# A 64-byte row instead of an 8-byte row in the first mixture's token table

## The chip, the cores and the metric

The kernel runs on one core of a Trainium2 chip. The metric is device time in microseconds (us) from launch to end. A core has five engines that run their own instruction queues and wait for each other by semaphores: PE (matmul and transposes), DVE (vector), ACT (activations, copies out of PSUM), POOL (GpSimd: element work, and the indirect DMAs, which gather or scatter rows by a list of indices), and SP, which here only starts plain DMAs. All DMAs of a core, whoever starts them, are carried by the same 16 DMA engines. On-chip memory has 128 partitions (SBUF for tiles, PSUM for matmul results); DRAM holds inputs, outputs and the two tables that this document is about.

## What is computed

Attention inside chunks of 64 positions, then two mixtures of 8 experts on the 4608 rows that it leaves. Cut to what matters:

```
x = attention(q, k, v)                        # 8 x 8 heads x 576 x 64, softmax in chunks of 64
x = x.transpose(0, 2, 1, 3).reshape(4608, 512)

# first mixture: every token goes to one expert
logits = x @ w_gate + modality_bias[modality_id]        # 4608 x 8
e_idx = argmax(logits); gate_w = softmax(logits)[e_idx]
out[e_idx == e] = gate_w * (relu(x[e_idx == e] @ w1[e]) @ w2[e])

# second mixture: only tokens with x @ w_skip > 0, the others are passed on
```

w1 is 8 x 512 x 1024 and w2 is 8 x 1024 x 512, both in float32.

## The kernel before

The program has three stages on one time line. **Attention** takes tiles of 128 tokens, 36 of them, t = 0 to 35, some 5.5 us each. `load_qk` brings q and k for 256 tokens in a DMA each (or two, at the edge of a batch), up to four pairs of tiles ahead, into two buffers; `load_v` brings v for a batch of 576 tokens (4.5 tiles), one DMA for each head, into one of two buffers (`g.v0` and `vt1`), two heads in each tile. All of these are started by SP, in the order of the program, so a load whose buffer isn't free yet holds those behind it. POOL reorders q and k (`reorder`, L445), PE transposes them (L453), forms scores (L482), transposes the exponentials (L508) and multiplies by v (`emit_av`, L517), after which DVE divides (`emit_norm`, L527 to L533). Every four tiles the finished rows are stored to DRAM by SP (L648, 1 MB).

Beside the tiles, and dripped in between their instructions, `route` sends each group of four tiles (512 tokens, groups gi = 0 to 8) through the first mixture's gate. Its product is a table in DRAM, `g.tab[0]`. It has a slot for each place in each expert's list: `g.NR` = 8 x 4608 + 256 = 37120 rows of two 32-bit numbers, the token's index and its gate as float bits. A token's slot is the expert's base (e x 4608) plus its rank among the tokens of that expert so far, so tokens of one expert fill slots that follow each other. `tables` (L157) first fills both tables with the index 65536, which later gathers skip; this is put on SP's queue in one of the first tiles. Then `route` writes index and gate of 4 x 128 tokens into a tile `row` (128 partitions x 4 x 2) and scatters them by four indirect DMAs of 128 rows each, started by POOL (L588), 36 in all. A `row` tile comes from a pool with two buffers.

**The first mixture's steps** read the table: `load_ids_at` (L323) fetches 256 consecutive slots, row by row, into an `ids` tile, POOL gathers the 256 rows of x that they name (L334), PE runs the two products (L364, L1095) and the results are scattered back (L1002). The first expert's w1 is loaded and split already during attention (L615 to L625), its w2 at the end of it (L1285, split on ACT and DVE in L980 and L982). While the first mixture runs, its outputs are routed for the second, with a table of the same shape, `g.tab[1]`, scattered at L268. **The second mixture's steps** read that one.

What sets the order around the change: SP's queue in program order for the two fills, the loads and the stores; POOL's queue in program order for the element work of `reorder` and the scatters. There is no planner.

Of the kernel before, what the change touches and what calls it, by code (L numbers as in the profile page):

```python
# [11 lines left out]
I32 = mybir.dt.int32  # L12
# [8 lines left out]
P = 128  # L21
E = 8
OOB = 65536.0
# [108 lines left out]
def setup_late(nc, g, tmp, modality_id, modality_bias, w_gate2, w_skip):  # L132

    NT, NTILE, DM = g.NT, g.NTILE, g.DM
    md = tmp.tile([NTILE, P, 2], I32, name="md")
    nc.gpsimd.dma_start(
        out=md, in_=modality_id.bitcast(I32).rearrange("(t p w) -> t p w", p=P, w=2)
    )
    b01 = tmp.tile([P, 2, E], F32, name="b01")
    nc.gpsimd.dma_start(  # L140
        out=b01.rearrange("p m e -> p (m e)"),
        in_=modality_bias.rearrange("m e -> (m e)").unsqueeze(0).to_broadcast([P, 2 * E]),
    )
    wsm = tmp.tile([P, 4, E + 1], F32, name="wsm")
    nc.gpsimd.dma_start(out=wsm[:, :, 0:E], in_=w_gate2.rearrange("(a p) e -> p a e", p=P))
    nc.gpsimd.dma_start(
        out=wsm[:, :, E:E + 1], in_=w_skip.rearrange("(a p o) -> p a o", p=P, o=1)
    )


    blank = tmp.tile([P, g.NR // P, 2], I32, name="blank")
    nc.gpsimd.memset(blank[:, :, 0], int(OOB))
    nc.gpsimd.memset(blank[:, :, 1], 0)

    def tables():
        for t in g.tab:
            nc.sync.dma_start(out=t.rearrange("(p n) c -> p n c", p=P), in_=blank)  # L157

    nop = lambda: None

    mf = tmp.tile([NTILE, P], F32, name="mf")

    def bias():
        pm = g.ps_l.tile([P, P], F32, tag="l", name="pm")
        nc.tensor.transpose(pm[:, 0:NTILE], mf, g.ident[0:NTILE, 0:NTILE])
        m = tmp.tile([P, NTILE, 2], F32, name="m")
        nc.vector.tensor_copy(m[:, :, 1], pm[:, 0:NTILE])
        nc.vector.tensor_scalar(
            out=m[:, :, 0], in0=m[:, :, 1], scalar1=-1.0, scalar2=1.0, op0=ALU.mult, op1=ALU.add
        )  # L170
        t0 = tmp.tile([P, NTILE, E], F32, name="t0")
        sh = [P, NTILE, E]
        for i, dst in ((0, t0), (1, g.bias)):
            nc.vector.tensor_tensor(
                out=dst,
                in0=m[:, :, i:i + 1].to_broadcast(sh),
                in1=b01[:, i:i + 1, :].to_broadcast(sh),
                op=ALU.mult,
            )
        nc.vector.tensor_tensor(out=g.bias, in0=g.bias, in1=t0, op=ALU.add)  # L180

    def rows():

        pr = g.ps_l.tile([P, DM], F32, tag="l", name="pr")
        for a in range(4):
            nc.tensor.transpose(pr[0:E + 1, a * P:(a + 1) * P], wsm[:, a, :], g.ident)
        rw = tmp.tile([E + 1, DM], F32, name="rw")
        nc.scalar.copy(rw, pr[0:E + 1, :])
        nc.scalar.dma_start(out=g.rows, in_=rw)

    g.late = [lambda: nc.vector.tensor_copy(mf, md[:, :, 0])] + g.late + [tables, nop, bias, nop, nop, nop, rows]


# [127 lines left out]

def load_ids_at(nc, g, which, dst, r):
    return nc.sync.dma_start(  # L323
        out=dst, in_=g.tab[which][bass.ds(r, 256), :].rearrange("(h p) c -> p h c", p=P)
    )


# [45 lines left out]
def attention(ctx, tc, g, q, k, v, w_gate, w1, out, small):  # L373
# [3 lines left out]
    nc = tc.nc  # L377
# [21 lines left out]
    ps_t, ps_l, rt_p = g.ps_t, g.ps_l, g.rt  # L399
# [154 lines left out]
    def route(gi, wait=3, wait2=1):  # L554
        for _ in range(wait):
            yield
        ps = ps_l.tile([P, 4, NA, 32], F32, tag="l", name="ps_l2")
        for t in range(4):
            nc.tensor.transpose(ps[:, t].rearrange("p a e -> p (a e)"), g.lsb[:, t * P:(t + 1) * P], ident)
        yield  # L560
        lgt = rt_p.tile([P, 4, E], F32, tag="lgt", name="lgt")
        nc.vector.tensor_reduce(
            out=lgt, in_=ps[:, :, :, 0:E].rearrange("p t a e -> p t e a"), axis=AX.X, op=ALU.add,
        )
        yield
        nc.vector.tensor_tensor(out=lgt, in0=lgt, in1=g.bias[:, 4 * gi:4 * gi + 4, :], op=ALU.add)
        row = rt_p.tile([P, 4, 2], I32, tag="row", name="row")
        nc.gpsimd.tensor_copy(row[:, :, 0], g.tokid[:, 4 * gi:4 * gi + 4])
        yield
        hot = yield from gate_argmax(nc, g, rt_p, lgt, 4, row[:, :, 1:2].bitcast(F32))  # L570
        for _ in range(wait2):
            yield
        ps = ps_l.tile([P, 5, E], F32, tag="l", name="ps_r")
        ranks_mm(nc, g, ps, hot, 4)
        yield
        pos = rt_p.tile([P, 4], F32, tag="pos", name="pos")
        yield from ranks(nc, g, rt_p, ps, hot, 4, g.carry[0], pos)
        posi = rt_p.tile([P, 4], I32, tag="posi", name="posi")
        nc.vector.tensor_copy(posi, pos)
        yield  # L580
        if gi == GP:
            yield from pick(nc, g, 0)
            jobs.extend(first_jobs())
        if gi == NG - 2:
            yield from snap(nc, g, 0)
        sc = []
        for i in range(4):
            b = nc.gpsimd.indirect_dma_start(  # L588
                out=g.tab[0], out_offset=IOff(ap=posi[:, i:i + 1], axis=0),
                in_=row[:, i, :], in_offset=None, bounds_check=g.NR - 1, oob_is_err=False,  # L590
            )
            sc.append(apart(tc, b, sc + (g.eids if gi > GP else [])))
            if gi < NG - 1:
                yield
                yield
        if gi == NG - 1:
            yield from g.control(0)
        if gi > GP:
            g.scat += sc
        if gi == NG - 2:  # L600
            early_ids(nc, g, 0, g.idsE[1], 256)
# [110 lines left out]
    for t in range(NTILE):  # L712
# [19 lines left out]
        if t == NTILE - 3:  # L732
            nc.sync.dma_start(
                out=g.v0[:, 0:(E + 1) * DM],
                in_=g.rows.rearrange("e d -> (e d)").unsqueeze(0).to_broadcast([P, (E + 1) * DM]),
# [197 lines left out]
def experts(ctx, tc, g, w, out, tail):  # L933
# [37 lines left out]
    def load_ids(which, j):  # L971
        load_ids_at(nc, g, which, g.ids[j % g.NID], reg(g.ints[which], j, 1, g.NR - 256))
# [378 lines left out]
@with_exitstack  # L1351
def kernel(
    ctx, tc, q, k, v, modality_id, w_gate, modality_bias, w1, w2,
    w_skip2, w_gate2, w12, w22, out, dbg=None,
):
    nc = tc.nc
    g = K()
    g.NT, g.DM = out.shape
    g.NTILE = g.NT // P
    g.NS = (g.NT + E * 255) // 256  # L1360
    g.VIRT = g.NS + 1
    g.NID = 5
    g.NR = E * g.NT + 256
    g.ints, g.ctl = {}, {}
    KD, KF = g.DM // P, w1.shape[2] // P
    dram = ctx.enter_context(tc.tile_pool(name="dram", bufs=1, space=DRAM))
    g.rows = dram.tile([E + 1, g.DM], F32, name="rows")
    g.tab = [dram.tile([g.NR, 2], I32, name=f"tab{i}") for i in range(2)]
    g.const = ctx.enter_context(tc.tile_pool(name="const", bufs=1))
    g.rt = ctx.enter_context(tc.tile_pool(name="rt", bufs=2))  # L1370
    keep = ctx.enter_context(tc.tile_pool(name="keep", bufs=1))
    g.ps_t = ctx.enter_context(tc.tile_pool(name="ps_t", bufs=3, space=PSUM))
    g.ps_l = ctx.enter_context(tc.tile_pool(name="ps_l", bufs=1, space=PSUM))
    g.w1s = keep.tile([P, 2, KD, KF * P], F32R, name="w1s")
    g.x4 = [keep.tile([P, 4, g.DM], F32, name=f"x4{i}") for i in range(3)]
    g.xe = keep.tile([P, 2, g.DM], F32, name="xe")
    g.xTb0 = keep.tile([P, 2, KD, 256], F32R, name="xTb0")
    g.xT4 = keep.tile([P, 4, 4 * P], F32, name="xT4")
    g.lsb = keep.tile([P, 4 * P], F32, name="lsb")

    g.v0 = keep.tile([P, q.shape[2] // 64 * q.shape[1] * (q.shape[3] + 1)], F32, name="v0")
    g.w2g = g.v0[:, 0:(E + 1) * g.DM].rearrange("p (e d) -> p e d", e=E + 1)
    g.lg = keep.tile([P, 2, E + 1], F32, name="lg")
    g.idsP = keep.tile([P, 2, 2], I32, name="idsP")
    g.row = keep.tile([P, 2, 2], I32, name="rowP")
    g.ids = [keep.tile([P, 2, 2], I32, name=f"ids{i}") for i in range(g.NID)]
    g.idsE = [keep.tile([P, 2, 2], I32, name=f"idsE{i}") for i in range(3)]
    with tc.manual_schedule():
        setup(tc, g)
        with ExitStack() as st:  # L1390
            tail = attention(
                st, tc, g, q, k, v, w_gate, w1, out, (modality_id, modality_bias, w_gate2, w_skip2)
            )
        experts(ctx, tc, g, ((w1, w2), (w12, w22)), out, tail)
# [31 lines left out]
```

## Time and profile before

| what | value |
|---|---|
| median of 3 runs | 992.92 us (992.51 to 997.83) |
| the profiled execution, as timed | 994.69 us |
| its span, first to last instruction | 993.0 us |
| busy: PE, DVE, ACT, POOL | 924.4, 646.2, 363.5, 309.2 us |
| mean granted TensorE clock | 0.974 of full |
| DMA | 119.38 MB in 121945 packets |

The profile cuts the span into 40 slices of 24.8 us; the attention stage is the first eight or nine. In a window's row stand, after the stretch and its length, the busy time of PE, of PE's weight loads (PEld), DVE, ACT and POOL, each with its number of instructions, and then the granted clock (1.00 is 2.4 GHz, 0.50 is 1.2 GHz), the mean busy share of the 16 DMA engines (over 1 where their packets overlap) and the GB/s that they moved. In a timeline's row stand the start, the length, the engine, the line, the operation, what it writes and reads, and in brackets how long the engine was idle before it and what ended that.

### The profile page before, as it was taken

To read this page: it belongs to the slowest core of one execution; us is meant where nothing else is said; L and a number is where in the kernel's file an instruction comes from. 1 tells how busy PE (TensorE), PEld (TensorE's weight loads), DVE (VectorE), ACT (ScalarE), POOL (GpSimd) and SP (SyncE) were. 2 spreads that over 40 slices of the span, in tenths; PEclk is the share of its full clock that TensorE was granted. 3 is DMA by queue.
4 is the path that set the end of the run, shared out by engine and by line. 5 is a ranking of instruction groups with operands and counts; after the bars stand their busy time and mean duration, and the time that the engine had idled before them with its cause. 6 is when DMAs were issued, how large, how long until landed. Compare 5 with 4: busy or idle time off the path is not lost. (4 is left out here: it accounts for less than half of the span.)

```text
span 993.0 us, 19577 instructions
## 1 busy us (share of the span) xinstructions
PE 924.4 (93%) x6757; PEld 816.3 (82%) x6757; DVE 646.2 (65%) x1837; ACT 363.5 (37%) x627; POOL 309.2 (31%) x284
## 2 busy tenths in 40 slices
PE   7887888889999999999889999988898999999996
PEld 6776767669999999888679999878797997897995
DVE  6576566558887777798687787788246365624361
ACT  6675667642212222341331121232126154514150
POOL 6464456424422222222232223220412211112210
PEclk9999898999999999999999999998999999999999
DMA  9999999584711111161101116000716546611500
GB/s 201 223 210 202 194 220 226 106 224 101 241 45 45 45 43 45 44 194 45 46 25 56 46 45 235 25 27 13 237 44 216 210 135 242 223 46 57 192 18 16
DMA packets 121945, 119.38 MB, mean 120 GB/s; under 512 B 56141, under 2 KB 93053, under 8 KB 121602
## 3 DMA queue, kind: packets, MB, share of 16 engines
q1 hardware_dynamic: 106192, 82.21, 33.2%
q0 software_dynamic: 14464, 34.17, 10.6%
q8 instruction: 85, 1.39, 0.7%
q14 instruction: 130, 1.06, 0.4%
q10 hardware_dynamic: 1074, 0.54, 0.2%
HBM read 96.37 MB, written 26.38 MB: 124 GB/s over the span
## 5 line engine op out<-in xcount | busy, mean ns | idle before, releaser
L1095 PE MATMUL p<-w2s,hT 128*128 128x512 f32 x1392 | 326.3, 391 | 0.0
L1095 PEld LDWEIGHTS p<-w2s,hT 128*128 128x128 f32 x1392 | 257.7, 188 | 51.9 <-DVEq L1203 0.2
L364 PE MATMUL p<-xTb,w1s 128*128 128x256 f32 x2064 | 263.2, 286 | 12.2 <-DVEq L1316 5.3
L364 PEld LDWEIGHTS p<-xTb,w1s 128*128 128x128 f32 x2064 | 254.7, 193 | 17.3 <-DVE w1s L982 6.2
L1012 DVE CUSTOM_DVE_ANT_0 x<-x,v 128x512 f32<-128x512 f32 x333 | 209.0, 686 | 47.7 <-ACT x L995 37.7
L1002 POOL DMA_INDIRECT out_dram<-x,ids x56 | 62.1, 1110 | 270.4 <-DVE x L998 205.7
L1061 ACT ACTIVATE hT<-p 128x512 fp32r<-128x512 f32 x86 | 51.4, 598 | 210.2 <-PE p L364 202.7
L268 POOL DMA_INDIRECT tab<-rowP,posi x38 | 40.6, 1069 | 222.8 <-DVE idsP L1111 175.6
L1062 DVE SCALAR_TENSOR_TENSOR hT<-p,hT 128x512 fp32r<-128x512 f32 x86 | 58.8, 686 | 65.6 <-ACT hT L1061 42.1
L334 POOL DMA_INDIRECT x<-out_dram,ids x68 | 76.7, 1128 | 56.5 <-issue 28.8
L364 PE MATMUL p1t<-xTb,w1s 128*128 128x256 f32 x696 | 88.1, 283 | 0.0
L364 PEld LDWEIGHTS p1t<-xTb,w1s 128*128 128x128 f32 x696 | 85.2, 191 | 1.7 <-issue 1.7
L995 ACT ACTIVATE x<-p,ids 128x512 f32<-128x512 f32 x33 | 22.7, 688 | 145.1 <-PE p L1095 141.7
L464 ACT COPY kb<-ps_t 64x512 f32<-64x512 f32 x70 | 44.0, 628 | 52.9 <-PE ps_t L453 52.5
L982 DVE TENSOR_TENSOR w2s<-r,w2s 128x512 fp32r<-128x512 f32 x88 | 56.8, 686 | 5.0 <-ACT w2s L980 5.0
L588 POOL DMA_INDIRECT tab<-row,posi x36 | 36.5, 1015 | 69.4 <-issue 28.3
L980 ACT CAST w2s<-r 128x512 fp32r<-128x512 f32 x88 | 51.0, 619 | 16.7 <-issue 6.4
L350 DVE TENSOR_TENSOR xTb<-px,xTb 128x512 fp32r<-128x512 f32 x70 | 44.9, 681 | 11.1 <-ACT xTb L349 10.3
L998 DVE SCALAR_TENSOR_TENSOR x<-p,ids,x 128x512 f32<-128x512 f32 x23 | 17.2, 747 | 53.4 <-PE p L1095 48.6
L527 DVE TENSOR_SCALAR rs<-o_ps 128x8 f32<-128x8 f32 x36 | 6.0, 166 | 67.3 <-PE o_ps L517 67.2
L982 DVE TENSOR_TENSOR w1s<-r,w1s 128x1024 fp32r<-128x1024 f32 x40 | 46.4, 1221 | 2.5 <-ACT w1s L980 2.2
L482 PE MATMUL sc<-kb,Tq 128*64 128x128 f32 x576 | 42.0, 287 | 5.9 <-DVE r_d L203 2.5
(217 smaller groups left out, 1110.4 us busy)
## 6 DMA issues: line engine op xcount, KB each, us to landing
r<-in_moe_w_dram SPq DMA_DIRECT2D x18, 2048.0 KB, 10.2
out_dram<-x SPq DMA_DIRECT2D x9, 1024.0 KB, 9.3
k<-in_k_dram SPq DMA_DIRECT2D x11, 512.0 KB, 6.8
q<-in_q_dram SPq DMA_DIRECT2D x11, 512.0 KB, 8.8
vt<-in_v_dram SPq DMA_DIRECT2D x32, 144.0 KB, 7.3
r<-in_moe_w_dram POOLq DMA_DIRECT2D x2, 2048.0 KB, 15.4
v<-in_v_dram SPq DMA_DIRECT2D x24, 144.0 KB, 7.3
v<-rows SPq DMA_DIRECT2D x1, 2304.0 KB
```

The costliest lines, as they stand in the source:

```text
L334: return [nc.gpsimd.indirect_dma_start(out=x[:, h, :], out_offset=None, in_=src, in_offset=IOff(ap=ids[:, h, 0:1], axis=0), bounds_check=s ...
L350: nc.vector.tensor_tensor(out=t[:, 1, :, h * P:(h + 1) * P], in0=ps, in1=o.bitcast(F32), op=ALU.subtract)
L364: nc.tensor.matmul(ps, w1s[:, b, kk, f * P:(f + 1) * P], xt[:, a, kk, :], start=(i == 0), stop=(i == 3 * KD - 1),)
L464: eng(kb[u % 2][64 * j:64 * j + 64, sl, j, :].rearrange("p a (c r) -> p a r c", r=2), ps[64 * j:64 * j + 64],)
L482: nc.tensor.matmul(out=ps[64 * c:64 * c + 64, a, :, :], lhsT=T_[u][:, a, cs], rhs=kb[u % 2][:, a, :, cs], start=True, stop=True,)
L980: hi(s[:, 0, kk, :], r[:, kk, :])
L982: eng.tensor_tensor(out=s[:, 1, kk, :], in0=r[:, kk, :], in1=s[:, 0, kk, :].bitcast(F32), op=ALU.subtract)
L1002: b = nc.gpsimd.indirect_dma_start(out=out, out_offset=IOff(ap=ids[:, h, 0:1], axis=0), in_=o[:, h, :], in_offset=None, bounds_check=NT - ...
L1012: nc.vector.tensor_tensor_reduce(out=junk[i % 2], in0=x2[:, h, :], in1=w2g[:, i, :], scale=1.0, scalar=0.0, op0=ALU.mult, op1=ALU.add, acc ...
L1061: nc.scalar.activation(out=o, in_=ps, func=AF.Relu)
L1062: nc.vector.scalar_tensor_tensor(out=l, in0=ps, scalar=0.0, in1=o.bitcast(F32), op0=ALU.max, op1=ALU.subtract)
L1095: nc.tensor.matmul(ps, hT[:, a, f, h * P:(h + 1) * P], w2s[:, b, f, :], start=(f == 0 and i == 0), stop=(f == KF - 1 and i == 2),)
```

## The change

The first table's rows get 16 numbers instead of 2, 64 bytes instead of 8. The second table stays as it is. Four things follow from that in the code.

- The fill of the first table writes 37120 x 64 bytes = 2.38 MB instead of 0.30 MB. Its source is a smaller tile, `blank0` (29 rows of 16 numbers in each partition), that the DMA reads ten times over.
- Four more memsets on POOL: two for `blank0`, one for each of two `row4` tiles.
- The scatters of `route` take whole rows of 64 bytes from `g.row4`, two fixed tiles used in turn; the numbers 2 to 15 of a row stay zero.
- `load_ids_at` fetches the first two numbers of each row.

```
+    n = g.NR // P
+    m = next(i for i in range(10, 0, -1) if n % i == 0)
+    blank0 = tmp.tile([P, n // m, 16], I32, name="blank0")
+    nc.gpsimd.memset(blank0, 0)
+    nc.gpsimd.memset(blank0[:, :, 0], int(OOB))
+    for t in g.row4:
+        nc.gpsimd.memset(t, 0)
+
     def tables():
-        for t in g.tab:
-            nc.sync.dma_start(out=t.rearrange("(p n) c -> p n c", p=P), in_=blank)
+        nc.sync.dma_start(
+            out=g.tab[0].rearrange("(p m n) c -> p m (n c)", p=P, m=m),
+            in_=blank0.rearrange("p n c -> p (n c)").unsqueeze(1).to_broadcast([P, m, n // m * 16]),
+        )
+        nc.sync.dma_start(out=g.tab[1].rearrange("(p n) c -> p n c", p=P), in_=blank)
...
-        out=dst, in_=g.tab[which][bass.ds(r, 256), :].rearrange("(h p) c -> p h c", p=P)
+        out=dst, in_=g.tab[which][bass.ds(r, 256), 0:2].rearrange("(h p) c -> p h c", p=P)
...
-        row = rt_p.tile([P, 4, 2], I32, tag="row", name="row")
+        row = g.row4[gi % 2]
...
-    g.tab = [dram.tile([g.NR, 2], I32, name=f"tab{i}") for i in range(2)]
+    g.tab = [dram.tile([g.NR, (16, 2)[i]], I32, name=f"tab{i}") for i in range(2)]
...
+    g.row4 = [keep.tile([P, 4, 16], I32, name=f"row4{i}") for i in range(2)]
```

No instruction of PE, DVE or ACT is added, removed or moved. On SP the two fills keep their place. This is SP's queue around them before, and then with the change (`blank` and `blank0` are the source tiles, `tab` the tables, `k`, `q`, `vt` the loads):

```order
L425 DMA k<-in_k_dram 128x8x128
L425 DMA q<-in_q_dram 128x8x128
L157 DMA tab_58<-blank 128x580
L157 DMA tab_59<-blank 128x580
L425 DMA k<-in_k_dram 96x8x128
```

```order
L437 DMA k<-in_k_dram 128x8x128
L437 DMA q<-in_q_dram 128x8x128
L165 DMA tab_58<-blank_357 1280x1x464
L169 DMA tab_59<-blank 128x580
L437 DMA k<-in_k_dram 96x8x128
```

The first fill is now 1280 runs of 464 numbers, ahead of the same loads. On POOL four memsets come between the constants and the first `reorder` (before, then with the change):

```order
L146 DMA wsm<-in_moe_w_skip_dram 128x4x1
L152 MEMSET blank 128x290
L153 MEMSET blank 128x290
L445 TENSOR_TENSOR rk<-k,zero 128x8x2x64
L445 TENSOR_TENSOR rq<-q,zero 128x8x2x64
```

```order
L146 DMA wsm<-in_moe_w_skip_dram 128x4x1
L152 MEMSET blank 128x290
L153 MEMSET blank 128x290
L159 MEMSET blank_357 128x464
L160 MEMSET blank_357 128x29
L162 MEMSET row_87 128x64
L162 MEMSET row_88 128x64
L457 TENSOR_TENSOR rk<-k,zero 128x8x2x64
```

Everything behind them on POOL stands in the order of before; a scatter's row there reads 37120x16 instead of 37120x2.

## Rows read from the trace of the kernel before

**Rows 1.** The page's 40 slices of 24.8 us: DMA share in tenths, GB/s.

```profile
DMA  9999999584711111161101116000716546611500
GB/s 201 223 210 202 194 220 226 106 224 101 241 45 45 45 43 45 44 194 45 46 25 56 46 45 235 25 27 13 237 44 216 210 135 242 223 46 57 192 18 16
```

**Rows 2.** DMA issues of the whole run: number, KB each, median us to landing.

```profile
tab<-blank SPq DMA_DIRECT2D x2, 290.0 KB, 5.8
tab<-row,posi POOLq DMA_INDIRECT x36, 6.6
```

**Rows 3.** Timeline of POOL: a reorder, and two of the 36 scatters.

```profile
51.31 1.89 POOL L445 TENSOR_TENSOR rq<-q,zero 128x1024 f32<-128x1024 f32 x1 [0.19 <-POOL rk L445]
...
58.73 1.08 POOL L588 DMA_INDIRECT tab<-row,posi  x1 [5.39 <-issue]
...
131.87 0.97 POOL L588 DMA_INDIRECT tab<-row,posi  x1 [0.30 <-issue]
```

**Rows 4.** Windows of the attention stage; the last three columns are PEclk, DMA share, GB/s.

```profile
64.00:66.00 2.00, 2.00 (x24) 1.48 (x20) 0.03 (x1) 1.98 (x5) 1.75 (x1) 1.00 1.06 79
66.00:69.00 3.00, 2.31 (x31) 1.58 (x28) 1.45 (x5) 0.97 (x2) 2.23 (x4) 1.00 1.10 306
72.00:76.00 4.00, 2.37 (x41) 2.22 (x38) 3.90 (x11) 1.82 (x5) 1.79 (x2) 1.00 1.20 136
94.00:100.00 6.00, 3.54 (x50) 3.15 (x46) 5.78 (x16) 2.33 (x6) 1.59 (x2) 0.86 1.39 122
134.00:137.00 3.00, 3.00 (x31) 1.83 (x31) 1.13 (x2) 2.90 (x6) 2.68 (x3) 1.00 0.80 41
186.00:191.00 5.00, 5.00 (x72) 4.66 (x71) 3.61 (x15) 4.26 (x9) 1.43 (x3) 1.00 0.89 83
212.00:215.00 3.00, 3.00 (x44) 2.68 (x44) 1.94 (x9) 0.50 (x2) 0.00 (x0) 1.00 0.59 33
```

**Rows 5.** Windows of the two fills at work, and of the stretch behind them.

```profile
42.40:45.70 3.30, 3.30 (x40) 2.32 (x40) 2.58 (x6) 2.63 (x6) 2.69 (x2) 1.00 1.07 333
49.50:52.00 2.50, 2.50 (x30) 2.16 (x27) 2.45 (x6) 1.27 (x3) 2.31 (x2) 1.00 0.30 60
```

**Rows 6.** Timeline of PE, matmuls: one without a wait, then those that waited.

```profile
58.52 0.66 PE L453 MATMUL ps_t<-ident,rk 128*128 128x128 f32 x4
...
66.95 0.44 PE L517 MATMUL o_ps<-v,pt 128*64 128x130 f32 x4 [0.69 <-DMA v<-in_v_dram]
...
88.14 0.30 PE L517 MATMUL o_ps<-vt,pt 128*64 128x130 f32 x1 [1.42 <-DMA vt<-in_v_dram]
...
89.62 0.43 PE L517 MATMUL o_ps<-vt,pt 128*64 128x130 f32 x2 [1.04 <-DMA vt<-in_v_dram]
...
119.22 0.70 PE L517 MATMUL o_ps<-v,pt 128*64 128x130 f32 x4 [3.06 <-DMA v<-in_v_dram]
...
144.30 0.30 PE L517 MATMUL o_ps<-vt,pt 128*64 128x130 f32 x1 [2.23 <-DMA vt<-in_v_dram]
...
197.25 0.43 PE L517 MATMUL o_ps<-vt,pt 128*64 128x130 f32 x1 [4.45 <-DMA vt<-in_v_dram]
...
221.64 1.93 PE L548 MATMUL ps_l<-xT,wg 128*32 128x512 f32 x8 [3.20 <-ACT xT L543]
```

**Rows 7.** Timeline of ACT: the first split of w2 at the end of attention.

```profile
219.97 1.14 ACT L980 CAST w2s<-r 128x512 fp32r<-128x512 f32 x2 [3.93 <-DMA r<-in_moe_w_dram]
```

**Rows 8.** Windows cut at changes of PE's granted clock.

```profile
66.00:118.80 52.80, 42.74 (x494) 35.24 (x490) 33.48 (x80) 33.18 (x61) 30.22 (x25) 0.97 1.07 199
118.80:125.70 6.90, 6.48 (x52) 5.85 (x54) 3.23 (x12) 2.37 (x5) 0.00 (x0) 0.51 1.20 229
197.30:200.80 3.50, 3.50 (x24) 3.17 (x25) 2.29 (x8) 0.06 (x1) 1.28 (x2) 0.51 0.23 86
```

**Rows 9.** Timeline of POOL: a memset of `blank`, and the reorder behind the memsets.

```profile
16.15 0.36 POOL L152 MEMSET blank<- 128x290 int32 x1
...
27.68 1.89 POOL L445 TENSOR_TENSOR rk<-k,zero 128x1024 f32<-128x1024 f32 x1 [10.87 <-DVE jcol L94]
```

## The prediction

> **What bounds the kernel now.** I read the page's 40 slices first. The DMA engines are full in the first seven slices, at some 210 GB/s, and mostly idle behind the ninth [rows 1]: whatever the change does through DMA traffic, it does in the attention stage, the first 225 us. From there on the two mixtures run on PE and scatter nothing into the first table; they only fetch it, in as many fetches as before. So a gain or a loss made in attention moves the end by the same amount, and none is made behind it.
>
> Next I read the windows of that stage at the grain of a few us. The rate isn't even. From 66 to 69 us it is 306 GB/s, with the DMA share over 1. In the other windows it falls to 79, 136, 122, 41, 83 and 33 GB/s, and in most of them the share is still near or above 1: the engines hold packets that don't finish [rows 4]. What these windows have in common I found on POOL's timeline. Each lies a few us behind scatters into the first table: the one from 134 behind a scatter at 131.87, the one from 64 behind that at 58.73 (its rows landed late, as the median of 6.6 us from issue to landing also says) [rows 2 to 4]. The same holds for the other four. I saw no such hole in this stage ahead of the first scatter. My reading is that 128 rows of 8 bytes hold up the memory: since an expert's slots follow each other, up to eight of them share 64 bytes, and writes that each take a part of the same piece have to wait for each other, and what queues behind them on the 16 engines waits too. That is inferred from order in time, not shown.
>
> The last view is PE's timeline, for what a hole costs. PE's waits for a DMA in this stage are few and all of one kind: attention's product waits for v of the next batch, 0.69, 1.42 + 1.04, 3.06, 2.23 and 4.45 us. A sixth, 3.20 us, is charged to ACT, which for 3.93 us waited for w2 of the first expert [rows 6, 7]. Sum: 16.1 us. v comes just in time, so a DMA hole ahead of it is a PE wait. And a wait costs twice: behind the 3.06 us wait PE's granted clock is 0.51 (the 1.2 GHz level) for 6.9 us, behind the 4.45 us one for 3.5 us [rows 8].
>
> **The change part by part.** *The fill.* The first table takes 2.38 MB in place of 0.30, so 2.08 MB more on SP's queue, at 39.5 us, ahead of loads that are needed soon. The two fills of before ran at 333 GB/s [rows 5]: 2.08 / 0.333 = 6.2 us of DMA time. The upper bound is the stage's rate of some 210 GB/s [rows 1], 9.9 us; I take 6.2, since it is the same kind of run (some 2 KB long) to the same place. Of it, some is free: from 49.5 to 52 us the DMA share is only 0.30 [rows 5], so 2.5 x 0.70 = 1.75 us of room. Net: loads behind it are 4.45 us late. For q and k that is hidden: POOL is done with its reorder at 53.2 us, and PE takes the first block of that pair at 58.52 without a wait [rows 3, 6], a cover of 5.3 us; without it the 4.45 us would fall on PE. For v of the third batch there is none: PE already waits for it at 66.95.
>
> *The scatters.* 36 of them, 128 rows each. The bytes grow from 1 to 8 KB each, 0.29 MB in all, or 1.4 us of DMA time at 210 GB/s spread over 180 us, so nothing. The number of rows stays, and POOL's time for one (1.08 and 0.97 us [rows 3]) with it. What may go is the hole behind them. Lost time in a hole is its length times (1 - its rate / 306): 1.5, 2.2, 3.6, 2.6, 3.6 and 2.7 us in the six windows of rows 4, 16.2 us. The bound on one side is nothing, on the other all of it. A 64-byte row has its 64 bytes to itself, if the table starts on such a boundary, so by my reading all goes; I take it so, and keep the other end for the rivals.
>
> *Where the gain lands.* The v wait at 66.95 gets 4.45 us of fill, less the 1.5 us of the hole at 64: +3.0 us. As PE is then 3.0 us late itself, later loads have that much more time. The wait at 88 (2.46) has the 2.2 us hole at 72 before it, that at 119 (3.06) the 3.6 us at 94, that at 144 (2.23) the 2.6 us at 134, that at 197 (4.45) the 3.6 us at 186, and that at 221 (3.20) the 2.7 us at 212. Taking the smaller of each pair: 2.2 + 3.06 + 2.23 + 3.6 + 2.7 = 13.8 us gained.
>
> *The clock.* PE issued 494 matmuls in 52.8 us at a clock of 0.97, 9.36 per us; in the slow stretches 52 in 6.9 (7.54 per us) and 24 in 3.5 (6.86) [rows 8]. A long one thus costs 6.9 x (1 - 7.54 / 9.36) = 1.3 us, a short one 0.9. There are two long ones behind v waits (at 118.8 and, alike, at 146.1) and one short: 3.5 us gained if the waits go. But the 3.7 us wait that now stands at 67 earns a long one: 1.3 us lost.
>
> *The rest.* Four memsets on POOL: the known one takes 0.36 us for 290 elements, so 464 + 29 + 2 x 64 some 0.8 us, in an idle stretch of 10.87 us [rows 9]. The `row4` tiles alternate as the pool's two buffers did. The fetches of ids have as many rows as before; they are started three steps ahead. The first scatter has to wait for the fill, which ends by 42.4 + 2.67 / 0.333 = 50.4 us, ahead of 58.73. All nothing.
>
> *Sum.* +3.0 + 1.3 - 13.8 - 3.5 = -13.0 us. I don't take it in full: where PE no longer waits for v, DVE, ACT or POOL, which run the same tiles in step with it, are late next now and then. I keep three quarters, -10 us; that quarter is a choice. The profiled execution took 994.7 us, so 984.7; the median of the runs is 1.8 us under that execution, so 983.
>
> *A rule that speaks against it.* The Trainium skill, page "DMA: Bandwidth & Descriptors", section Specifications, puts the smallest transfer for line rate at 512 bytes and says that below it the DMA engine does a read-modify-write. By it a row of 64 bytes is treated as one of 8 is, the holes would stay, and the third and fourth cases below would hold. No run here yet shows 64-byte rows; that the holes follow 8-byte rows agrees with it as well as with mine.
>
> **The rivals.** *Half gone.* If the writes hold each other up over longer pieces than 64 bytes, the holes shrink but stay. At half: +3.7 + 1.3 - 6.9 - 1.8 = -3.7 us, and three quarters of the gain again: about 990. For it: nothing here says how long the piece is.
>
> *The holes stay, and the fill is paid back.* The change then doesn't do what it is built for. The fill costs 4.45 us at 66.95, but PE's lateness gives the later loads 4.45 us more time, and the waits at 88 to 144 (7.75 us) shrink by what the DMA engines gain back in their own pauses: 994 to 996. For it: it needs only that some of the five later v batches come with slack.
>
> *Slower: the holes stay, and the fill is paid in full.* The mechanism is the fill ahead of the third batch of v at 66.95: 4.45 us of wait and 1.3 us of clock, 5.8 us, nothing given back, as v is just in time again in every batch: 999. At 210 GB/s for the fill it is 9.9 - 1.75 + 1.3 = 9.5 us, 1002. It decides if holes of today's size are still there and v for 66.95 comes more than 4 us later.
>
> **How the numbers follow.** By 0.5% (5 us, about what a measurement of this kernel can tell from no change) faster means under 988, slower above 998. Chances: holes gone 0.58 (976 to 989, at 983); half gone 0.15 (986 to 992); stay and paid back 0.16; stay and paid in full 0.11. Faster takes 0.57 of the first and 0.05 of the second, 0.62; slower is the fourth, 0.11; the rest, 0.27, is within 0.5%. The range goes from 975 (13 us gained on the median and 5 for waits on other engines that follow v) to 997, which leaves out the fourth case and a little at the low end.
>
> **What would show it right or wrong.** Right: in the attention stage of the changed kernel no window of 2 us or more behind a scatter is under 150 GB/s with work queued; the median landing of the 36 scatters falls under 6.6 us although the traffic around them is the same; PE's v waits behind the third batch add up to less than 4 us, and the clock's drops behind them are gone; the wait at about 67 us grows to 3 or 4 us. Wrong: holes of 40 to 130 GB/s still follow the scatters (the rule's case), or the holes are gone and PE waits as long for DVE or ACT (then attention isn't bound by DMA, and the quarter that I took off was too small), or the wait at 67 us is far over 4 us (the fill is slower than 333 GB/s).

## The result, and the profile after

The changed kernel takes 967.9 us (median of 4 runs, 965.6 to 971.8) against 995.4 us for the kernel before beside it: ratio 0.972, 95% interval 0.967 to 0.978. That is 27 us less; 10 were forecast, and the time lies 7 us below the low end of the range. The profiled execution took 967.2 us with a span of 965.6 us.

The page's 40 slices, now of 24.1 us, answer [rows 1]: DMA share in tenths, then GB/s.

```profile
DMA  9999996836111111341111134001626456512400
GB/s 216 275 271 229 239 248 164 276 119 237 46 48 55 47 46 56 121 124 49 34 47 46 46 118 150 25 28 27 229 77 244 150 192 234 193 46 93 164 18 16
```

The same share of DMA time now moves 216 to 275 GB/s in the first six slices, where it moved 194 to 223; the second of them also holds the larger fill. The DMA issues answer [rows 2] (number, KB each, median us to landing).

```profile
tab<-blank SPq DMA_DIRECT2D x1, 2320.0 KB, 12.1
tab<-row,posi POOLq DMA_INDIRECT x36, 3.9
```

A scatter lands after 3.9 us in place of 6.6, with eight times the bytes. Windows of the changed kernel answer [rows 4] (last three columns: PEclk, DMA share, GB/s).

```profile
68.00:72.00 4.00, 4.00 (x26) 3.34 (x26) 3.97 (x4) 0.60 (x1) 3.98 (x4) 0.50 1.12 314
94.00:98.00 4.00, 4.00 (x60) 3.66 (x62) 3.23 (x13) 2.54 (x6) 0.00 (x0) 1.00 1.33 213
128.00:132.00 4.00, 4.00 (x54) 3.66 (x54) 2.52 (x8) 2.42 (x5) 1.03 (x2) 1.00 1.16 320
...
175.00:177.00 2.00, 2.00 (x25) 1.83 (x24) 1.65 (x5) 1.87 (x4) 0.00 (x0) 1.00 0.59 121
```

The last is the lowest of the stage. I counted windows of 2 us, one starting each us from 58 to 218 us, with a DMA share of 0.55 or more and under 150 GB/s: 33 before, down to 33 GB/s; 4 after, none under 121. Of these, 21 before and none after have a DMA share of 0.9 or more, so that the engines were full. The experiments are compared by the same count. PE's timeline answers [rows 6].

```profile
64.69 0.44 PE L529 MATMUL o_ps<-v,pt 128*64 128x130 f32 x4 [2.12 <-DMA v<-in_v_dram]
...
66.67 0.70 PE L529 MATMUL o_ps<-v,pt 128*64 128x130 f32 x4 [1.53 <-DMA v<-in_v_dram]
```

These are the only two waits of PE for a DMA in the stage; all others of [rows 6] are gone, as is ACT's 3.93 us [rows 7]. The waits summed by line say the same: of PE, us in total, times, longest. Before, from 62 to 231 us:

```profile
PE o_ps L517 <- DMA vt<-in_v_dram: 9.1, 4, 4.4
PE ps_r L236 <- DVE r_oh L218: 6.0, 3, 3.4
PE o_ps L517 <- DMA v<-in_v_dram: 3.8, 2, 3.1
PE ps_l L548 <- ACT xT L543: 3.2, 1, 3.2
PE sc L482 <- DVE r_d L203: 2.5, 1, 2.5
PE sc L482 <- DVE pk_ei L302: 1.4, 1, 1.4
```

After, from 58.5 to 205 us:

```profile
PE ps_r L248 <- DVE r_oh L230: 3.9, 2, 3.4
PE o_ps L529 <- DMA v<-in_v_dram: 3.7, 2, 2.1
PE sc L494 <- DVE r_d L215: 2.9, 2, 1.5
PE sc L494 <- DVE r_z L259: 0.8, 1, 0.8
```

**Where the 27.4 us went.** Windows that begin at the same instruction (the output multiply of tile 8) and hold the same 1538 matmuls divide the gain; the columns are length, PE busy with its matmuls, four more engines, PEclk, DMA share, GB/s. Before:

```profile
62.00:231.00 169.00, 142.52 (x1538) 118.73 (x1535) 103.38 (x276) 101.01 (x184) 80.32 (x66) 0.92 0.93 187
231.00:283.00 52.00, 52.00 (x342) 46.93 (x341) 43.43 (x178) 11.38 (x21) 19.74 (x20) 1.00 0.54 162
283.00:993.00 710.00, 676.42 (x4331) 606.37 (x4329) 458.90 (x1290) 209.24 (x352) 176.62 (x160) 0.99 0.28 93
```

After:

```profile
58.50:205.00 146.50, 134.65 (x1538) 112.08 (x1535) 103.41 (x277) 100.63 (x184) 81.83 (x66) 0.97 0.88 222
205.00:257.00 52.00, 52.00 (x342) 46.92 (x341) 43.33 (x178) 11.29 (x21) 19.66 (x20) 1.00 0.48 164
257.00:965.60 708.60, 675.64 (x4330) 606.14 (x4329) 459.32 (x1290) 209.24 (x352) 182.41 (x160) 0.99 0.28 93
```

The first window is 22.5 us shorter. PE's idle time in it fell from 169.00 - 142.52 = 26.5 to 11.9 us, 14.6 us less; its busy time for the same matmuls fell by 7.9 us, which goes with the clock (0.92 to 0.97). Tile 8 itself stands 3.5 us earlier, and the last 710 us are 1.4 us shorter: 3.5 + 22.5 + 0.0 + 1.4 = 27.4. This is one pair of profiles; a second pair stands at the end of the experiments, and not every share comes out there.

### The profile page after: what moved, and what is told of

Read it like the earlier page. It is cut to its first block, busy times and chain, and to the rows that moved or that the text cites. A ratio compares the mean times of both kernels' runs of the same rounds, so it can differ in the third digit from the quotient of the medians.

```text
span 965.6 us, 19576 instructions
## 1 busy us (share of the span) xinstructions
PE 912.1 (94%) x6757; PEld 806.4 (84%) x6757; DVE 647.1 (67%) x1837; ACT 363.0 (38%) x627; POOL 316.5 (33%) x288
## 3 DMA queue, kind: packets, MB, share of 16 engines
q8 instruction: 85, 1.39, 0.7%
## 5 line engine op out<-in xcount | busy, mean ns | idle before, releaser
L1014 POOL DMA_INDIRECT out_dram<-x,ids x56 | 67.6, 1207 | 267.0 <-DVE x L1010 203.0
L362 DVE TENSOR_TENSOR xTb<-px,xTb 128x512 fp32r<-128x512 f32 x70 | 44.9, 682 | 11.2 <-ACT xTb L361 10.3
L361 ACT CAST xTb<-px 128x512 fp32r<-128x512 f32 x70 | 37.6, 591 | 19.4 <-PE px L359 19.4
```

The source lines that it names most:

```text
L362: nc.vector.tensor_tensor(out=t[:, 1, :, h * P:(h + 1) * P], in0=ps, in1=o.bitcast(F32), op=ALU.subtract)
L1014: b = nc.gpsimd.indirect_dma_start(out=out, out_offset=IOff(ap=ids[:, h, 0:1], axis=0), in_=o[:, h, :], in_offset=None, bounds_check=NT - ...
```

## The experiments

Theory S: rows that share a piece of memory hold each other's writes up, and everything behind them. Its rival P: it is the size of the write. The cuts of code show the lines that matter and leave out the rest of each edit. The medians of the kernel before ran from 991.7 to 1001.8 us between chips, so ratios to it are what is compared.

**8 bytes at a pitch of 64.** The table of the change; only its first 8 bytes are written.

```
-        nc.vector.tensor_copy(posi, pos)
+        nc.vector.tensor_scalar(out=posi, in0=pos, scalar1=8.0, scalar2=None, op0=ALU.mult)
-                out=g.tab[0], out_offset=IOff(ap=posi[:, i:i + 1], axis=0),
-                in_=row[:, i, :], in_offset=None, bounds_check=g.NR - 1, oob_is_err=False,
+                out=g.tab[0].rearrange("n (a c) -> (n a) c", c=2), out_offset=IOff(ap=posi[:, i:i + 1], axis=0),
+                in_=row[:, i, 0:2], in_offset=None, bounds_check=8 * g.NR - 1, oob_is_err=False,
```

> The changed kernel, but each scatter writes only the 8 bytes that are used, into rows that still lie 64 bytes apart (the list of positions is multiplied by 8, the table is filled as in the change). Theory S (writes that share a 64-byte piece hold each other up): no two writes share a piece, so the holes stay away: 965 to 972 us, no window of 2 us behind a scatter under 150 GB/s with the DMA share near 1. Rival P (any write of part of a 64-byte piece is slow, shared or not): the holes are back and the larger fill is paid too: 993 to 1001 us.

972.75 us, ratio 0.982 (0.976 to 0.988), just over what theory S gave. Four windows under 150 GB/s in place of 33, down to 88 GB/s, none of them with a DMA share of 0.9 or more. PE's waits of this kernel for a DMA, from 58 to 262 us:

```profile
PE o_ps L529 <- DMA v<-in_v_dram: 1.9, 2, 1.0
```

So the pitch cures, not the size of the write: P falls, and S stands so far as it says that the rows must lie apart.

**Rows of 16 and of 32 bytes.** `g.tab[0]`, `row4` and `blank0` have 4 numbers to a row (or, in the second kernel, 8) in place of 16.

```
-    g.tab = [dram.tile([g.NR, (16, 2)[i]], I32, name=f"tab{i}") for i in range(2)]
+    g.tab = [dram.tile([g.NR, (4, 2)[i]], I32, name=f"tab{i}") for i in range(2)]
```

> The changed kernel with rows of 16 bytes: four rows share 64 bytes, the fill is 0.59 MB. Theory S with a hole as long as the number of rows that share a piece: half of the holes' time of the kernel before is left, 978 to 984 us. Rival P: every write is still a part of a piece, so the holes are as before, 991 to 996 us.

> The changed kernel with rows of 32 bytes: two rows share 64 bytes, the fill is 1.19 MB. Theory S: a quarter of the holes' time is left and the fill costs about 2 us less at tile 9 than with 64 bytes: 969 to 975 us. Rival P: as before plus some 2 us of fill, 992 to 998 us. If 32 bytes are the memory's own piece, there is no hole at all: 963 to 968 us.

16 bytes: 976.89 us, ratio 0.985 (0.979 to 0.991), 12 windows, down to 73 GB/s. 32 bytes: 969.75 us, ratio 0.979 (0.973 to 0.985), 3 windows, none under 108. The holes shrink at 16 and are all but gone at 32, not first at 64. It is the windows that say so. The times alone don't: 976.89 us lies under the 978 to 984 of theory S, and 969.75 us lies where a quarter of the holes was to be left, not at the 963 to 968 of a piece of 32 bytes. The kernel with 16 bytes has the fixed `row` tiles, the kind of fill and the fetch of the change, and keeps holes, so none of these is the cure. One hole that is left with 16 bytes, on POOL's timeline and in the windows:

```profile
121.67 1.02 POOL L600 DMA_INDIRECT tab<-row,posi  x1 [0.15 <-DVE pk_er L307]
123.00 0.98 POOL L600 DMA_INDIRECT tab<-row,posi  x1 [0.30 <-issue]
```

```profile
124.00:126.00 2.00, 2.00 (x18) 1.01 (x16) 0.42 (x1) 0.00 (x0) 1.41 (x2) 1.00 0.88 88
126.00:128.00 2.00, 1.56 (x18) 1.18 (x16) 0.43 (x1) 0.38 (x1) 0.86 (x2) 1.00 0.61 129
```

**8 bytes at a pitch of 32**, in the manner of the first experiment, `scalar1=4.0` and a table of 8 numbers to a row. It tells a piece that must not be shared (S32) from one that must be filled (F32).

> As e1_8_in_64, but with rows 32 bytes apart: 8 bytes written into each piece of 32, so two rows share 64 bytes and none share 32. After the runs of 16 and 32 bytes there are two readings. S32 (the piece that must not be shared has 32 bytes): no holes, 967 to 975 us. F32 (the piece has 64 bytes, but a write of a full 32 bytes is not disturbed): holes about as with 16-byte rows, 976 to 982 us.

965.46 us, ratio 0.974 (0.970 to 0.978); 2 windows, none under 134; scatters land after 4.5 us. F32 falls: 8 bytes alone in 32 are enough. The Trainium skill, page "DMA: Bandwidth & Descriptors", section Specifications, has everything under 512 bytes read, modified and written; these runs show that this by itself makes no holes here, since 8 bytes at a pitch of 32 leave as good as none. The Trainium skill's page "Collectives: The Full Stack", section "Rules for kernel authors", wants buffers aligned to 32 bytes to prevent a read-modify-write by the hardware; 32 is the size found here, but no run shows that this is the reason.

The packet records of the traces say it more sharply than the windows. Of the DMA packets of 256 bytes or more that start between 57 and 232 us, these last over 2 us: 59 and 23 in the two profiles of the kernel before, 13 with rows of 16 bytes, 3 and 6 in the two profiles of 8 bytes at a pitch of 32, none with rows of 32 bytes, with 8 bytes at a pitch of 64 or in the change. From 5 to 55 us, ahead of the scatters, none of these kernels has one. Most of the long packets belong to the loads and stores that SP started: the price of the small rows falls on other transfers.

What is shown is the pitch. That two rows in one piece of 32 bytes are the reason is argued: wherever the holes went, an expert's rows also lay farther apart in memory, and it may be how densely the writes fall that counts. The same 8-byte pitch with the slots in another order would tell; it was not run.

**The fill alone.** The kernel before, with 2.08 MB more written on SP's queue at the place of the fill.

```
+        nc.sync.dma_start(
+            out=g.extra.rearrange("(p m n) c -> p m (n c)", p=P, m=10),
+            in_=blank0.rearrange("p n c -> p (n c)").unsqueeze(1).to_broadcast([P, 10, n // 10 * 14]),
+        )
```

> The kernel before (8-byte rows), with 2.08 MB more written to a DRAM tensor that nobody reads, just ahead of the two fills on SP's queue, in runs of 1624 bytes. It is the change's cost without its gain. My sum said +4.3 us at tile 9 (3.0 without the hole at 64 us, 1.3 of clock), or 5.8 with that hole: 997 to 1001 us if it is paid in full. Rival (paid back, since later loads have more time): 992 to 996 us.

994.75 us, ratio 1.003 (0.999 to 1.006). The interval reaches from nothing to 6 us, so the time doesn't tell whether the fill is paid. PE's timeline does; it shows the price at tile 9, and that the later waits for v shrink from the 12.2 us of [rows 6] to 2.7:

```profile
71.91 0.66 PE L525 MATMUL o_ps<-v,pt 128*64 128x130 f32 x4 [3.68 <-DMA v<-in_v_dram]
...
73.20 0.70 PE L525 MATMUL o_ps<-v,pt 128*64 128x130 f32 x4 [0.63 <-DMA v<-in_v_dram]
...
95.48 0.41 PE L525 MATMUL o_ps<-vt,pt 128*64 128x130 f32 x2 [0.77 <-DMA vt<-in_v_dram]
...
145.61 0.30 PE L525 MATMUL o_ps<-vt,pt 128*64 128x130 f32 x1 [0.34 <-DMA vt<-in_v_dram]
...
197.42 0.30 PE L525 MATMUL o_ps<-vt,pt 128*64 128x130 f32 x1 [1.61 <-DMA vt<-in_v_dram]
```

With the holes in place the fill is paid back: tile 9 stands 6.5 us later than in the kernel before, the last tile 0.7 us earlier. (The second profile of the kernel before stands 4.1 us ahead of its first at the last tile, so this is sure to some 4 us only.)

**Twice the scatters.** The kernel before with each scatter repeated into a second 8-byte table, and the change with each repeated into a second 64-byte table (nobody reads the second table).

```
+            b2 = nc.gpsimd.indirect_dma_start(
+                out=g.dup, out_offset=IOff(ap=posi[:, i:i + 1], axis=0),
+                in_=row[:, i, :], in_offset=None, bounds_check=g.NR - 1, oob_is_err=False,
+            )
```

> The kernel before, with each of the 36 scatters followed by the same one into a second table of 8-byte rows that nobody reads: twice the 8-byte writes. Theory S: the holes of the attention stage double (long packets there cost some 27 us of the 16 engines' time more than in the changed kernel; now some 54), and attention ends 20 to 30 us later than before: 1010 to 1025 us, less what POOL's own 36 x 1.3 us adds (see dup64). Rival (what was gained came from another place than the writes, such as the fixed row tiles or the fetches): the doubling costs no more than dup64's does over the changed kernel.

> The changed kernel, with each of the 36 scatters followed by the same one into a second table of 64-byte rows that nobody reads. The control to dup8: the same 47 us of POOL's time, no writes that share a piece. Theory S: no holes; POOL was busy 310 us of the span and has room, so 968 to 976 us. Rival (each scatter costs by its number of writes, whatever they share): holes come in here too, 980 to 990 us.

With 8 bytes: 1019.7 us, ratio 1.030 (1.025 to 1.035), 38 windows, down to 28 GB/s. With 64: 986.56 us, ratio 0.994 (0.992 to 0.997), 4 windows, but over the change by 15 us in the profiles and 19 in the medians. The second missed its forecast: POOL's time for 36 more scatters isn't hidden. PE's waits there, from 57.7 us on, are for DVE:

```profile
PE sc L494 <- DVE r_z L259: 9.4, 3, 6.5
```

Ahead of the longest of these waits one of DVE's operations, 0.17 us in the median, takes 7.54 us. It ends at 121.92 us, as POOL's element work does at 121.89, which behind six scatters goes on without a pause from 114.30 us. So DVE seems to wait for POOL. First DVE's timeline, then the last of POOL's run:

```profile
114.38 7.54 DVE L239 TENSOR_SCALAR r_sm<-r_sm 128x4 f32<-128x4 f32 x1
```

```profile
119.99 1.90 POOL L457 TENSOR_TENSOR rq<-q,zero 128x1024 f32<-128x1024 f32 x1
```

The two kernels lie 33 us apart, but 25 to 27 of that lie between the kernels that they were made from. Doubling costs 27 us with 8-byte rows and some 19 with 64-byte rows, so the 8 bytes themselves cost some 6 to 8 us more the second time. Theory S had the holes doubling, and they didn't: 38 windows against 33 and, in the second profile, 21; 61 packets of over 2 us against 59 and 23. Why the added 8-byte scatters cost so much less than the first ones stays open. PE's waits of the 8-byte kernel from 60.9 to 290 us:

```profile
PE o_ps L517 <- DMA v<-in_v_dram: 8.4, 3, 6.5
PE px L347 <- DMA x<-out_dram,ids: 7.6, 1, 7.6
PE sc L482 <- DVE r_z L247: 7.5, 2, 4.9
PE ps_l L548 <- ACT xT L543: 7.4, 1, 7.4
```

`px` is the first mixture's fetch of tokens by the table, behind attention.

**Both tables at 32 bytes.** As with 32 bytes above, and the second mixture's table too.

```
-    g.tab = [dram.tile([g.NR, (16, 2)[i]], I32, name=f"tab{i}") for i in range(2)]
+    g.tab = [dram.tile([g.NR, (8, 8)[i]], I32, name=f"tab{i}") for i in range(2)]
```

> Both tables with rows of 32 bytes (the second one's scatters too): a version that might beat the change. The second table is scattered while DMA is mostly idle, so theory S sees no wait that could go there: 966 to 972 us, the same as with 32 bytes in the first table alone. Rival (the second table's scatters hold up the fetches of ids and rows in the mixtures): a gain of 3 us or more on 969.75, under 967 us.

974.05 us, ratio 0.983 (0.979 to 0.987), 2 us over what I had expected: no gain over the first table alone. The second table's scatters go out where the DMA engines have room. They land sooner all the same: after 2.2 us in the median, where the kernel before has 3.6. For the first table the median is 5.6 us here, and 5.9 with the doubled 64-byte rows, both without holes: a landing close to the 6.6 of before is no sign of them by itself.

**The change, the 32-byte pitch and a late batch of v, side by side.** The last adds to the change 4.16 MB on SP's queue just ahead of the last two loads of v for tile 18.

```
+        if t == 17:
+            nc.sync.dma_start(
+                out=g.extra.rearrange("(p m n) c -> p m (n c)", p=P, m=20),
+                in_=g.blank0.rearrange("p n c -> p (n c)")[:, 0:nn * 14].unsqueeze(1).to_broadcast([P, 20, nn * 14]),
+            )
```

> The change as it is, for a second look on the same chip as the two kernels beside it. If the 27 us are the change's and not one chip's, the ratio to the kernel before lies again between 0.967 and 0.978 (960 to 971 us), the PE waits for v stay gone but for some 3 to 4 us at about 65 us, and the last tile of attention ends 20 us or more ahead of the kernel before. If a few us of it were start-up luck of one profile, the time is 970 to 975 us.

> The version with 8 bytes written at a pitch of 32 bytes, once more, on the same chip as the change. Piece of 32 bytes: no holes, the same time as the change to within 4 us, on the early side if on any, since its fill is half as long (1.19 MB in place of 2.38, some 3 us less at the wait near 65 us). If the earlier 965 us stood for a real gain over the change, it is 2 to 4 us faster than it again; if that was one chip, they differ by less than 1 us.

> The change and, added, 4.16 MB written to a table of its own that nobody reads, on SP's queue between the loads of k, q (tile 16) and the last two loads of v for tile 18. It prices one late v batch where no holes are. In the change's trace these two loads land at 103.8 and 105.3 us and PE needs them at 111 us without a wait: 5.7 us of cover. At 333 GB/s the write takes 12.5 us: a wait of some 7 us at about 111 us. Theory C (a late batch costs its wait and about two thirds of it again at half clock, and nothing is given back, since no later wait is left that could shrink): 7 + 4 to 5, so 11 to 12 us over the change, and a stretch or two at half clock behind the wait. The prediction's price (1.3 us for a long stretch): 7 + 1.3, about 8 us over the change. Given back (as in the kernel before with a fill alone): 0 to 3 us over the change, the tiles behind catching up.

The change: 973.88 us, ratio 0.975 (0.971 to 0.979), again 25 to 28 us under the kernel before beside it; the time in us is over what I had expected, as that kernel is slower on this chip. The last tile of attention ends 18.5 and 14.4 us ahead of the two profiles of the kernel before, where I had expected 20 or more. The 32-byte pitch: 972.25 us, 0.973 (0.969 to 0.977), 7 windows, down to 102 GB/s, none with a DMA share of 0.9 or more: no version here is measurably faster than the change. The late batch: 996.91 us, 0.996 (0.993 to 0.998), 23 us over the change, which none of the three expectations (up to 12 us) had. Its wait on PE's timeline:

```profile
126.13 0.70 PE L529 MATMUL o_ps<-v,pt 128*64 128x130 f32 x4 [10.33 <-DMA v<-in_v_dram]
```

Tiles 17 to 23, first in the change beside it, then with the late batch:

```profile
106.70:136.50 29.80, 26.04 (x318) 21.38 (x318) 23.12 (x69) 22.04 (x40) 16.00 (x13) 1.00 1.00 225
```

```profile
113.10:156.20 43.10, 27.83 (x319) 23.32 (x319) 24.57 (x69) 22.45 (x40) 16.09 (x13) 0.88 1.09 248
...
115.80:126.20 10.40, 0.07 (x3) 0.10 (x4) 1.61 (x5) 1.31 (x4) 0.01 (x1) 0.74 1.11 265
```

The stretch is 13.3 us longer: 11.5 us of idle time and 1.8 us of busy time. The wait was sized too small (7 us), and nothing is given back behind it: the last tile is still 20.4 us later, of which 6.4 us were there ahead of the write. For the clock, 1.8 us is near the prediction's 1.3 and far from the two thirds of theory C, which falls: about half of the slow stretch lies inside the wait (PEclk 0.74 while PE has nothing to do). Some 10 of the 23 us lie outside these tiles, and I can't say why; the price of a late batch is read from the stretch alone.

**The kernel before, profiled again.**

> The kernel before, profiled a second time, to tell what of the 27 us is the change's from what one profile happens to show. In the first profile tile 8's output multiply starts at 62.0 us and the stretch from there to the mixture's first product of w2 (230.7 us) takes 168.7 us, against 58.5 and 146.1 us in the changed kernel. If the holes are the kernel's own, the second profile shows them behind the same scatters, PE waiting 13 to 20 us in all for v and w2, and that stretch at 165 to 172 us. If the first tiles' 3.5 us are luck of a run, tile 8 starts anywhere from 58.5 to 62 us; if they belong to the kernel before, at 61.5 us or later. If the waits for v were luck, the stretch is under 160 us.

992.6 us. The holes are its own (21 windows, down to 71 GB/s; landing again 6.6 us), and PE waits 14.5 us for v. Tile 8 stands at 61.1 us, which by what I had written counts for luck in the first tiles. And attention takes 161.2 us in place of 169, where I had expected 165 to 172; the time is no better for it. The windows say where it is lost:

```profile
61.10:222.30 161.20, 139.68 (x1538) 115.92 (x1534) 103.59 (x276) 100.81 (x184) 79.87 (x66) 0.94 0.96 195
222.30:281.30 59.00, 54.30 (x342) 47.85 (x341) 43.49 (x179) 11.63 (x21) 20.64 (x20) 0.97 0.55 144
```

The 342 matmuls behind attention take 59 us, not 52. PE's timeline there:

```profile
258.39 1.04 PE L347 MATMUL px<-ident,x 128*128 128x128 f32 x4 [2.83 <-DMA x<-out_dram,ids]
...
259.95 1.11 PE L347 MATMUL px<-ident,x 128*128 128x128 f32 x4 [0.52 <-DMA x<-out_dram,ids]
```

With `idsE` it is 4.8 us of waiting: the last scatters land, the ids are read from the table, the tokens are fetched by them, and PE turns them over. The last eight scatters (number, median us to landing), in this profile, in the first one of before, and in the change:

```profile
tab<-row,posi POOLq DMA_INDIRECT x8, 6.4
```

```profile
tab<-row,posi POOLq DMA_INDIRECT x8, 5.5
```

```profile
tab<-row,posi POOLq DMA_INDIRECT x8, 2.2
```

In the kernel before this chain is a second bound, close behind attention: when attention ran 8 us faster, the chain took 7 back. It does so with the fill alone too (3.2 us at `px`). In the change it is 3 to 4 us shorter at each scatter and no `px` waits, though attention ends 17 to 26 us earlier.

Beside this profile belongs the second one of the change, with the same two stretches:

```profile
58.80:208.00 149.20, 134.80 (x1538) 110.64 (x1535) 99.09 (x276) 100.93 (x184) 81.79 (x66) 0.98 0.84 217
208.00:261.00 53.00, 52.11 (x342) 46.44 (x341) 43.38 (x178) 11.13 (x21) 20.04 (x20) 1.00 0.47 161
```

The two come from different chips, so their spans don't give the gain, but they tell which shares of it hold. PE's waits for a DMA in the first stretch go from 14.5 to 1.8 us, 12.7 less (12.4 in the first pair). The busy time falls by 4.9 us, not 7.9. PE's waits for DVE rise from 5.9 to 9.2 us where they fell in the first pair. Tile 8 stands 2.3 us earlier, the 342 matmuls behind take 6.0 us less, and all that follows takes 3.3 us more.

## Why the prediction came out as it did

- *The reading of the holes.* Right in the main: they follow the 8-byte scatters, and they are worth most of the gain. It was inferred from order in time; the first experiment and the 32-byte pitch show that the pitch is the cause. That shared pieces are behind it stays argued. Wrong in size: 32 bytes are enough, so half of the change's row would have done. Two readings were loose. The window from 212 us starts 8 us behind its four scatters, though their rows landed only after 12.8 us. And one window ahead of the first scatter, from 28 to 30 us, is as slow (119 GB/s at a share of 0.59); none of the other three profiles of the two kernels has it.
- *The fill.* Right in kind. The wait near 67 us was forecast at 0.69 + 3.0 = 3.7 us and is 2.12 + 1.53 = 3.65 us in the first profile of the change, but 1.84 us in the second and 3.55 + 0.91 us with the late batch, behind the same fill, so there is luck in the match. The fourth case (paid in full, with holes) is spoken against by the waits in the fill alone; the third had its mechanism right.
- *Where the gain lands.* Right in kind, a little small. Forecast net of the fill: 10.8 us of waits for DMA. Measured: 16.1 to 3.7, 12.4 us. Taking the smaller of hole and wait was a little too careful; the count shows more windows under 150 GB/s than the six of [rows 4], and they may have added to the same waits, which I did not test.
- *The three quarters.* A choice without a row behind it, and as a cut it was wrong. PE's waits for DVE were to grow; they fell in the first pair of profiles, from 9.9 to 7.6 us, and grew by 3.3 us in the second. Either way the gain of the other terms was larger than forecast. Without that cut the forecast would have been 13 us.
- *The clock.* The step that failed most: net 2.2 us forecast, 7.9 measured in the first pair and 4.9 in the second. Two terms of it were too small. From [rows 8] I counted three slow stretches, 17.3 us. The window from 62 to 231 us holds three more, 27 us in all: two stand at waits of PE for DVE that I hadn't listed (2.46 us until 97.07, 3.40 us until 170.41), one at the 3.20 us that I had:

```profile
98.40:101.80 3.40, 3.40 (x25) 3.33 (x21) 1.90 (x6) 2.16 (x4) 0.00 (x0) 0.51 1.00 165
170.00:173.40 3.40, 2.99 (x27) 2.99 (x27) 3.37 (x9) 2.33 (x4) 1.27 (x1) 0.50 1.00 246
221.20:224.60 3.40, 2.96 (x13) 1.30 (x14) 2.60 (x5) 2.87 (x6) 2.67 (x3) 0.50 0.06 18
```

  After the change two are left, 10 us: one behind the waits for v near 66 us, one at a wait of 3.42 us for DVE. And I priced a slow us at 0.19 to 0.26 us by matmuls counted per us over a stretch that includes waits; the busy time gives 7.9 / (27 - 10) = 0.46 us, and in the second pair 4.9 / (20.4 - 6.8) = 0.36.
- *"None is made behind it".* Wrong for the kernel before: the chain behind attention takes back what attention gains, unless the scatters land sooner. Nor do the scatters into the first table end with attention: the last four start from 235.10 us on, 10 us behind the prediction's 225. The change shortened both, so no gain was lost.
- *What is left.* 13.0 forecast ahead of the cut, and 1.6 for waits on DMA, 2.3 for waits on DVE and 5.7 for the clock make 22.6, the window's 22.5. The 3.5 us ahead of tile 8 were in no step. Tile 2 is through at 31.6 us after and 34.9 before, ahead of the fill's effect and of any scatter; in the other profiles it ranges from 31.0 to 34.9 with wider rows and from 33.0 to 33.6 with 8 bytes. Whether the change has a part in it stays open. The forecast of 983 us also stood on a kernel before of 992.92 us; beside the change it took 995.38.

## What to carry to other kernels

When small rows are scattered to DRAM by index and neighbours go out close together, a pitch of 32 bytes was enough here, and the write need not fill it. Look for the price not in the scatter but in the rate of everything else on the DMA engines just behind it. And price a clock drop from PE's busy time over windows with equal matmul counts and from all the drops of the granted clock in the stage, not from the few that stand behind the waits one happens to list.

## What the runs showed of the hardware

- Behind scatters of 128 rows of 8 bytes, up to four of them in a stretch of 32 bytes, the DMA engines moved 33 to 136 GB/s for some us at DMA shares of 0.59 to 1.39; at 16 bytes 12 slow windows were left of 33 (21 in a second profile), at 32 bytes as good as none. 8 bytes alone in 32 bytes did as well as 32 written, in time.
- 38 scatters of the second table landed after 3.6 us with 8-byte rows and after 2.2 us with 32-byte rows, in a stage where DMA is mostly idle.
- A us at PE's lower clock level cost 0.36 to 0.46 us of busy time for the same matmuls in this mixture of small products; the half of a slow stretch that fell into a wait of 10.3 us left the price at 1.8 us for some 10 us of it.
- One operation of DVE that takes 0.17 us in the median took 7.54 us while POOL's element work ran without a pause, and ended with it. No run tests what held it up.
